# One decode block on one core: wq issued behind ACT's table load, and wider row spacing of two weights in DRAM

## The chip, the core and the metric

The kernel runs on one core of a Trainium2 chip. The metric is the device time of one execution in microseconds (us). All inputs lie in DRAM in layouts that the kernel's own preparation chooses; that preparation is not timed.

## What is computed

One token for each of four sequences passes through a block: a modulated layer norm, attention over the last 2,048 positions of a cache, a gated residual, a second modulated norm, and a gated feed-forward layer. The reference, cut to what matters:

```python
W = 2048                                     # from Sk = 8192
mod = silu(c) @ w_mod                        # (4, 6*512): sa, ca, ga, sb, cb, gb
h = layernorm(x) * (1 + ca) + sa
q = (h @ wq)                                 # 32 heads of 128
p = softmax(q @ k_cache[..., -W:, :].T * 128**-0.5)   # 8 groups of 4 heads share k and v
x = x + ga * ((p @ v_cache[..., -W:, :]) @ wo)
h = layernorm(x) * (1 + cb) + sb
x = x + gb * ((silu(h @ w1) * (h @ w3)) @ w2)
```

Everything is float32. The inputs are some 101 MB, nearly all of it weights and cache that are used once.

## The kernel before

All large inputs are loaded into one SBUF tensor, `ring`, of three slots (`slots`, lines 162 and 163) of 64 KiB per partition. What is loaded, in the order of the program:

- slot 0: `w_mod_a` (line 186), the columns of `w_mod` that the first norm needs, with x and c beside them: 128 rows of 4,128 floats, 16,512 bytes. Issued by SP, the first instruction of its queue.
- slot 1: `wq` (line 188): 128 rows of 16,144 floats, 64,576 bytes. Issued by ACT, the first instruction of its queue and its only transfer. The 240 columns of each row that do not fit beside `GUESTS` are loaded as eight small transfers, the `guests` (lines 202 to 204, 3 rows of 5,760 bytes each), into the tile `p_sb` by SP.
- slot 2: the keys and values of group 0, `kv_in[0]` (line 205), 128 rows of 65,536 bytes, by SP.
- then the other groups (`kv[1]` line 296, `kv[2]` line 329, the rest behind each `group(g)`), each into the slot that the work before has read, and at the end `wo` and the rest of `w_mod`, the last group, `w1`, `w3` and `w2`.

The helper `load` (line 174) issues one transfer per tensor; the source it is given decides the row spacing in DRAM. `Program` (line 44) records every operation with the tiles it touches; `emit` (line 79) derives the waits from these. The engines run their own operations in the order of the text. All operations of the kernel have line 59 in the profile, since `Program` issues them; they are told apart by tiles.

ACT's next instruction after the issue of wq is line 189, `preload_act_table_set`, which loads the table for Exp and Ln. Its first use is the Exp on c (line 240, tile `e`), which needs `w_mod_a`. From `w_mod_a` on, the norm, the modulation (`mod_columns`, `modulate`) and a transpose give `hT`; then the q projection (line 306 on, tiles `s_ps<-ring,hT`) needs `wq`, and `group(0)` (line 350) needs q and `kv_in[0]`.

`_layout` (line 493) lays the inputs out in DRAM. Rows of `w_mod_a` and `wq` stand there one directly behind the other, 16,512 and 64,576 bytes apart.

Of the kernel before, what the change touches and what calls it, by code (L numbers as in the profile page):

```python
# [9 lines left out]
P = 128  # L10
# [6 lines left out]
GUESTS = 240  # L17
# [130 lines left out]
def block_kernel(nc, w_mod_a, wq, guests, kv_in, wo_mod, last_k_wo, last_v, wo, w1, w3, w2, out):  # L148
# [7 lines left out]
    def sb(name, *shape):  # L156
        return nc.alloc_sbuf_tensor(name, (P, *shape), F32).ap()
# [5 lines left out]
    slots = [ring[:, n * 2 * HALF : (n + 1) * 2 * HALF] for n in range(3)]  # L163
# [10 lines left out]
    def load(dst, src, cuts=(0, 1), queue="sync"):  # L174
        step = src.shape[1] // cuts[-1]
        for lo, hi in zip(cuts[:-1], cuts[1:]):
            do(queue, "dma_start", dst[:, lo * step : hi * step], src[:, lo * step : hi * step])
        return dst[:, : src.shape[1]]
# [4 lines left out]

    first = load(slots[0], w_mod_a)
    wma, xt_sb, ct_sb = first[:, :4096], first[:, 4096:4112], first[:, 4112:]
    wq_t = load(slots[1], wq, queue="scalar")
    do("scalar", "preload_act_table_set", "natural_log_exp_and_others")
    kv = [None] * G  # L190


# [52 lines left out]
    xc, sq, h = (sb(n, P) for n in ("xc", "sq", "h"))  # L245
    ss, ln, r0, ve, a, r = (sb(n, 1) for n in ("ss", "ln", "r0", "ve", "a", "r"))
# [246 lines left out]
def _layout(i):  # L493
    import numpy as np

    def a(t):
        return np.ascontiguousarray(t)

    k = i["A_k_cache"][:, :, SK - W :, :].reshape(B, G, NT, 512, DH)
    v = i["A_v_cache"][:, :, SK - W :, :].reshape(B, G, NT, NC, P, DH)  # L500
    wm = i["w_mod"].reshape(4, P, 6, 4, P)
    xc = np.concatenate([i[n].reshape(B, 4, P).transpose(2, 1, 0).reshape(P, 16) for n in ("A_x", "c")], 1)
    w2 = i["B_w2"].reshape(14, P, D)
    wq = a(i["A_wq"].reshape(4, P, G, 512).transpose(1, 2, 0, 3)).reshape(P, 16384)
    guests = np.zeros((2, 12, 6, GUESTS), np.float32)
    for n, (at, lo, hi) in enumerate(GUEST_AT):
        for m in range(2):
            guests[m, lo:hi, n] = wq[at + 32 * m + lo : at + 32 * m + hi, 16384 - GUESTS :]
    wo = a(i["A_wo"].reshape(2, 4, R, P, D).transpose(0, 3, 1, 2, 4)).reshape(2, P, 8192)
    kv = np.concatenate([k.transpose(1, 4, 2, 0, 3).reshape(G, P, 8192), v.transpose(1, 4, 2, 0, 3, 5).reshape(G, P, 8192)], 2)  # L510
    return {
        "w_mod_a": np.concatenate([a(wm[:, :, :2].transpose(1, 0, 3, 2, 4)).reshape(P, 4096), xc], 1),
        "wq": a(wq[:, : 16384 - GUESTS]),
        "guests": guests.reshape(24, 6 * GUESTS),
        "kv_in": kv[: G - 1],
        "wo_mod": np.concatenate([wo[0], a(wm[:, :, 2:].transpose(1, 0, 3, 2, 4)).reshape(P, 8192)], 1),
        "last_k_wo": np.concatenate([kv[G - 1, :, :8192], wo[1, :, :4096]], 1),
        "last_v": a(kv[G - 1, :, 8192:]),
        "wo": a(wo[1, :, 4096:]),
        "w1": a(i["B_w1"].reshape(4, P, FF).transpose(1, 0, 2)).reshape(P, 4 * FF),  # L520
        "w3": a(i["B_w3"].reshape(4, P, FF).transpose(1, 0, 2)).reshape(P, 4 * FF),
        "w2": a(np.stack([w2[4 * j + c] for c, j in CHUNKS], 1)).reshape(P, NF * D),
    }
# [15 lines left out]
```

## Time and profile before

| | |
|---|---|
| time, median of 3 runs (lowest to highest) | 242.15 us (242.04 to 242.48) |
| span of the profiled execution | 240.8 us (1.35 us below the median of the runs) |
| TensorE busy | 148.7 us (62%) |
| VectorE, ACT busy | 56.3 us (23%), 24.1 us (10%) |
| bytes moved, mean rate over the span | 101.39 MB, 421 GB/s |

The span runs from the first to the last instruction in the profile; for the profiled execution itself the profile gives no other time, so the difference to the median of the runs is what lies around the span. PE is TensorE, DVE is VectorE, POOL is GpSimd, SP is the engine that issues most transfers; ACTq and SPq are the queues of ACT and SP, where transfers are issued. DMA share is the mean busy share of the core's 16 DMA engines. Busy shares are averages over stages with different limits, so the stages are read one by one below.

### The profile page before, as it was taken

The page shows a single profiled execution, that of the slowest core. Times are in us where ns is not written, and L with a number is a line of the kernel's source. Part 1 is how long each engine was busy: PE and PEld are TensorE (multiplying, and loading weights), DVE is VectorE, ACT ScalarE, POOL GpSimd, SP SyncE. Part 2 cuts the span into 40 slices and gives each one's busy share as a digit, 9 for nine tenths or more (in the row PEclk, how much of TensorE's full clock was granted, in tenths as well). Part 3 has the DMA queues.
Part 4 walks back from the last instruction along what each step waited for, and adds up shares of the span by engine and source line. Part 5 has one row for each costly group of instructions (what it writes and reads, how often), then busy time and mean ns, then how long its engine had stood idle before and what let it go on. Part 6 is the DMA issues. An engine that isn't in the chain of part 4 may idle for free.

```text
span 240.8 us, 2502 instructions
## 1 busy us (share of the span) xinstructions
PE 148.7 (62%) x1113; PEld 54.2 (22%) x1113; DVE 56.3 (23%) x141; ACT 24.1 (10%) x36; POOL 4.5 (2%) x12
## 2 busy tenths in 40 slices
PE   0000169982984962944867576667399719965876
PEld 0000133322322212201312222221042202422333
DVE  5000231034152024123132133130313104113210
ACT  2000000003003003001100300300200001320100
POOL 7000000000000000000000000000000000000000
PEclk9999997997696798879797799795759968995899
DMA  8999999999999999999999999999999999999994
GB/s 305 434 444 455 424 425 446 416 446 414 457 395 468 403 459 414 449 425 446 425 446 427 435 435 435 435 427 446 425 446 425 411 419 430 386 444 443 401 413 162
DMA packets 2937, 101.39 MB, mean 421 GB/s; under 512 B 472, under 2 KB 472, under 8 KB 880
## 3 DMA queue, kind: packets, MB, share of 16 engines
q1 hardware_dynamic: 2784, 92.99, 89.8%
q10 hardware_dynamic: 144, 8.27, 8.0%
q8 instruction: 8, 0.13, 0.2%
q14 instruction: 1, 0.01, 0.0%
HBM read 101.22 MB, written 0.03 MB: 420 GB/s over the span
## 4 chain that ended last, share of the span: by engine, by line
DMA 60%; PE 31%; DVE 5%; ACT 3%; issue 1%; ACTq 0%
DMA ring<-kv_in 33%; DMA ring<-w 16%; PE s_ps L59 14%; DMA ring<-w_mod_a 11%; PE bank L59 9%; PE o_ps L59 6%; DVE nm L59 3%; ACT p_sb L59 3%; PE a_ps L59 1%; DVE mod_a L59 0%; ACT work L59 0%; DVE p_sb L59 0%; DVE e L59 0%; DVE h L59 0%; DVE sq L59 0%
## 5 line engine op out<-in xcount | busy, mean ns | idle before, releaser
L59 PE MATMUL s_ps<-ring,qT 128*32 128x512 f32 x256 | 36.5, 722 | 20.3 <-DMA ring<-kv_in 13.3
L59 PE MATMUL bank<-ident,p_sb 128*128 128x128 f32 (+1 forms) x136 | 27.7, 353 | 30.8 <-ACT p_sb L59 30.7
L59 PE MATMUL o_ps<-ring,pT 128*16 128x512 f32 x256 | 38.4, 707 | 0.1
L59 PEld LDWEIGHTS bank<-ident,p_sb 128*128 128x128 f32 (+1 forms) x136 | 19.8, 178 | 52.5 <-ACT p_sb L59 31.7
L59 ACT ACTIVATE p_sb<-s_ps,nm 128x2048 f32<-128x2048 f32 (+1 forms) x11 | 16.5, 1501 | 139.7 <-DVE oT L59 104.1
L59 DVE TENSOR_REDUCE nm<-s_ps 128x1 f32<-128x2048 f32 x7 | 16.0, 2292 | 32.5 <-PE s_ps L59 32.5
L59 DVE COPY pT<-bank 128x64 f32<-128x64 f32 x32 | 7.2, 225 | 57.0 <-PE bank L59 57.0
L59 PEld LDWEIGHTS s_ps<-ring,qT 128*32 128x32 f32 x256 | 8.7, 129 | 46.9 <-issue 20.1
L59 PE MATMUL bank<-ident,xs 128*128 128x128 f32 x1 | 0.5, 476 | 27.8 <-POOL xs L59 27.8
L59 PE MATMUL s_ps<-ring,h2T 128*32 128x512 f32 (+1 forms) x64 | 9.0, 657 | 2.3 <-DMA ring<-w 2.3
L59 PE MATMUL s_ps<-ring,hT 128*32 128x512 f32 (+1 forms) x64 | 9.4, 705 | 0.0
L59 PEld LDWEIGHTS o_ps<-ring,pT 128*16 128x16 f32 x256 | 5.4, 99 | 11.9 <-issue 9.0
L59 DVE SCALAR_TENSOR_TENSOR o_own<-o_ps,rl,own 128x512 f32<-128x512 f32 x7 | 5.3, 751 | 11.1 <-PE o_ps L59 11.1
L59 PE MATMUL a_ps<-ring,oT 128*4 128x512 f32 x64 | 7.4, 592 | 0.0
L59 DVE TENSOR_REDUCE o_sum<-o_own 128x128 f32<-128x512 f32 x7 | 7.2, 1034 | 0.2
L59 PE MATMUL bank<-ring,sc 128*32 128x256 f32 (+1 forms) x64 | 6.9, 587 | 0.0
L59 PEld LDWEIGHTS bank<-ident,xs 128*128 128x128 f32 x1 | 0.2, 183 | 27.8 <-POOL xs L59 27.8
L59 DVE TENSOR_SCALAR e<-e 128x16 f32<-128x16 f32 x1 | 0.2, 175 | 23.3 <-ACT e L59 23.3
L59 DVE COPY qT<-bank 128x64 f32<-128x64 f32 x8 | 2.2, 280 | 12.4 <-PE bank L59 12.0
L59 DVE TENSOR_REDUCE mx<-s_ps 128x1 f32<-128x512 f32 x4 | 2.8, 692 | 9.0 <-PE s_ps L59 9.0
L59 PEld LDWEIGHTS s_ps<-ring,h2T 128*32 128x32 f32 x64 | 2.6, 130 | 7.3 <-issue 4.4
L59 PE MATMUL s_ps<-ring,hidT 128*32 128x64 f32 (+1 forms) x112 | 3.6, 274 | 0.3 <-DVE hidT L59 0.3
(97 smaller groups left out, 63.7 us busy)
## 6 DMA issues: line engine op xcount, KB each, us to landing
ring<-wq ACTq DMA_DIRECT2D x1, 8072.0 KB, 26.9
ring<-w SPq DMA_DIRECT2D x2, 3584.0 KB, 37.9
ring<-last_k_wo SPq DMA_DIRECT2D x1, 6144.0 KB, 30.1
ring<-last_v SPq DMA_DIRECT2D x1, 4096.0 KB, 39.5
ring<-w_mod_a SPq DMA_DIRECT2D x1, 2064.0 KB, 26.7
ring<-wo SPq DMA_DIRECT2D x1, 2048.0 KB, 41.8
ring<-w SPq DMA_DIRECT2D x1, 2048.0 KB, 43.1
ring<-w SPq DMA_DIRECT2D x1, 768.0 KB, 44.5
```

Of the source, the lines that this page charges most:

```text
L59: op = Op(engine, lambda: getattr(getattr(self.nc, engine), method)(*args, **kw), [])
```

## The change

Three things. On ACT the issue of `wq` moves from ahead of the table load to behind it. In DRAM the rows of `w_mod_a` are filled up with zeros to 5,120 floats, so that they begin 20,480 bytes apart, and those of `wq` to 17,408 floats, 69,632 bytes apart. The loads take the same 4,128 and 16,144 floats of each row as before, so the same bytes move into the same places.

```diff
-    first = load(slots[0], w_mod_a)
+    first = load(slots[0], w_mod_a[:, :4128])
     wma, xt_sb, ct_sb = first[:, :4096], first[:, 4096:4112], first[:, 4112:]
-    wq_t = load(slots[1], wq, queue="scalar")
     do("scalar", "preload_act_table_set", "natural_log_exp_and_others")
+    wq_t = load(slots[1], wq[:, : 16384 - GUESTS], queue="scalar")
...
+    def spaced(t, row):
+        return np.concatenate([t, np.zeros((P, row - t.shape[1]), np.float32)], 1)
...
-        "w_mod_a": np.concatenate([a(wm[:, :, :2].transpose(1, 0, 3, 2, 4)).reshape(P, 4096), xc], 1),
-        "wq": a(wq[:, : 16384 - GUESTS]),
+        "w_mod_a": spaced(np.concatenate([a(wm[:, :, :2].transpose(1, 0, 3, 2, 4)).reshape(P, 4096), xc], 1), 5120),
+        "wq": spaced(wq[:, : 16384 - GUESTS], 17408),
```

ACT's instructions at the start of the program, with + and - where the change differs from before (`e` is the Exp on c, `ring` the loaded inputs, `ln` the first norm):

```order
@@ -1,4 +1,4 @@
+L59 ACT_TABLE_LOAD
 L59 DMA ring<-wq 128x16144
-L59 ACT_TABLE_LOAD
 L59 ACTIVATE e<-ring 128x16
 L59 ACTIVATE ln<-bank,eps_t 128x1
```

The two first rows have changed places, and nothing else on ACT has moved.

SP's instructions at the start of the program, in the changed kernel:

```order
L59 DMA ring<-w_mod_a 128x4128
L59 DMA p_sb<-guests 3x1440 x8
L59 DMA ring<-kv_in 128x16384 x7
L59 DMA ring<-wo_mod 128x16384
```

They stand as they did before; so do those of TensorE, VectorE and GpSimd.

## Rows read from the trace of the kernel before

**Rows 1.** Page, chain that ended last: start us, us, what; first its shares.
```profile
DMA 60%; PE 31%; DVE 5%; ACT 3%; issue 1%; ACTq 0%
...
0.73 26.68 DMA ring<-w_mod_a
...
67.41 38.51 DMA ring<-kv_in
...
123.18 40.79 DMA ring<-kv_in
...
190.94 38.54 DMA ring<-w
```

**Rows 2.** Windows, two stretches of keys and values (first line: the columns).
```profile
core 0: us, PE busy (x) PEld busy (x) DVE busy (x) ACT busy (x) POOL busy (x), PEclk, DMA share, GB/s
47.25:66.60 19.35, 14.10 (x91) 5.49 (x92) 5.50 (x14) 2.65 (x3) 0.00 (x0) 0.82 1.00 434
...
144.00:163.35 19.35, 11.66 (x82) 4.23 (x82) 5.84 (x10) 2.06 (x2) 0.00 (x0) 0.91 1.00 431
```

**Rows 3.** Timeline of SP's issues to 70 us: start us, us, engine, line, operation.
```profile
8.95 40.08 SPq L59 DMA_DIRECT2D ring<-kv_in  x3
...
34.19 0.33 SPq L59 DMA_DIRECT2D ring<-kv_in  x1
...
48.70 0.33 SPq L59 DMA_DIRECT2D ring<-kv_in  x1
...
67.41 0.33 SPq L59 DMA_DIRECT2D ring<-kv_in  x1
```

**Rows 4.** Windows, the long middle and the last microseconds.
```profile
28.00:229.50 201.50, 139.81 (x945) 49.76 (x944) 51.26 (x118) 21.39 (x32) 0.00 (x0) 0.84 1.00 431
...
236.00:236.50 0.50, 0.50 (x8) 0.12 (x4) 0.00 (x0) 0.00 (x0) 0.00 (x0) 1.00 0.82 328
...
237.00:237.50 0.50, 0.47 (x35) 0.30 (x25) 0.00 (x0) 0.44 (x1) 0.00 (x0) 1.00 0.68 262
237.50:238.00 0.50, 0.50 (x36) 0.50 (x40) 0.00 (x0) 0.00 (x0) 0.00 (x0) 1.00 0.08 29
```

**Rows 5.** Windows, the start: first packets, then one turn of both queues per window.
```profile
1.50:2.50 1.00, 0.00 (x0) 0.00 (x0) 0.96 (x6) 0.93 (x1) 1.00 (x1) 1.00 1.05 264
2.50:3.50 1.00, 0.00 (x0) 0.00 (x0) 1.00 (x9) 0.00 (x0) 1.00 (x3) 1.00 2.64 1033
3.50:5.25 1.75, 0.00 (x0) 0.00 (x0) 0.88 (x4) 0.00 (x0) 1.52 (x3) 1.00 0.00 0
5.25:8.25 3.00, 0.00 (x0) 0.00 (x0) 0.00 (x0) 0.00 (x0) 0.00 (x0) 1.00 1.00 432
...
23.25:26.25 3.00, 0.00 (x0) 0.00 (x0) 0.00 (x0) 0.00 (x0) 0.00 (x0) 1.00 1.00 432
```

**Rows 6.** DMA issues: operation, KB each, median us from issue to landing.
```profile
ring<-wq ACTq DMA_DIRECT2D x1, 8072.0 KB, 26.9
...
ring<-w_mod_a SPq DMA_DIRECT2D x1, 2064.0 KB, 26.7
...
p_sb<-guests SPq DMA_DIRECT2D x8, 16.9 KB
```

**Rows 7.** Timeline of ACT to 30 us; in brackets idle time before, and its releaser.
```profile
0.73 0.39 ACTq L59 DMA_DIRECT2D ring<-wq  x1
1.15 1.28 ACT L59 ACT_TABLE_LOAD   x1 [1.15 <-PEq L532]
27.43 0.21 ACT L59 ACTIVATE e<-ring 128x16 f32<-128x16 f32 x1 [25.00 <-DMA ring<-w_mod_a]
```

**Rows 8.** Chain that ended last, 27 to 54 us: start of q projection and of scores.
```profile
27.43 0.22 ACT e L59
...
36.85 11.81 PE s_ps L59 x76
...
50.60 3.65 PE s_ps L59 x32
```

## The prediction

> **What bounds the kernel now.** I read the chain that ended last first. On the page it is DMA for 60% and TensorE for 31% of the span, and its long pieces are waits for a transfer: 26.68 us for w_mod_a, 38.51 and 40.79 us for two groups of keys and values, 38.54 us for w3 [rows 1]. Such a wait is longer than a transfer. One group is 128 rows of 65,536 bytes, 8.39 MB; the stretches of 19.35 us each move 434 and 431 GB/s with a DMA share of 1.00 [rows 2], so one group needs 8.39 MB / 434 GB/s = 19.3 us, and a wait of 38.5 us is a transfer standing behind another one. That says: the queue is never empty, and TensorE's pieces in the chain lie beside transfers that run anyway.
>
> The issues of SP show how deep the queue is [rows 3]. Its transfers run in order and one at a time from w_mod_a on. The group issued at 67.41 us lands at 67.41 + 38.51 = 105.92 us [rows 1]; counting back by 19.35 us per group, the earlier ones end at 86.6, 67.2 and 47.9 us. So the issue at 34.19 us had 13.7 us in hand before the queue would have run dry, the one at 48.70 us had 18.5 us, the one at 67.41 us had 19.2 us. From 28 us to 229.50 us the DMA share is 1.00 at 431 GB/s [rows 4], and only in the last 2 us do some engines run out of work [rows 4]. The end is therefore: the time at which the transfers reach full rate, plus their bytes at full rate, plus a short tail (last matmuls, two additions, the store of the result). The change moves no byte into or out of the total, so it can act in two ways only: through the rate, and through the first microseconds.
>
> **The first microseconds** [rows 5]. A row of these windows counts a packet where it starts. The window from 1.50 us holds 264 KB, the first row of w_mod_a (16,512 bytes) on each of 16 engines; the next holds 1,033 KB, the first row of wq (64,576 bytes) on each. Their shares, 1.05 and 2.64 over 1.00 us, are the mean time of one such packet: 1.05 and 2.64 us. After that each 3.00 us hold one row of both per engine (432 GB/s x 3.00 us = 1.30 MB = 16 x 81,088 bytes), split by bytes 0.61 and 2.39 us. The two queues thus take turns, row by row, and both transfers need all 8 turns: w_mod_a and wq land 26.7 and 26.9 us after their issues at 0.73 us [rows 6], although w_mod_a has a quarter of the bytes. The start is dear: 1.05 - 0.61 = 0.44 us and 2.64 - 2.39 = 0.25 us, together 0.69 us on a mean engine.
>
> **The change part by part.**
>
> *The issue behind the table load.* The two instructions of ACT swap places; nothing is added. Now the issue takes 0.39 us from 0.73 us and the table load 1.28 us from 1.15 us [rows 7]. Behind the load the issue begins near 0.73 + 1.28 = 2.0 us. What is queued behind it on ACT is only the Exp for silu(c), which waits for w_mod_a until 27.43 us [rows 7]. So the table load itself costs nothing, and the later wq is covered by w_mod_a: 8 rows of 0.61 us per engine keep all engines busy from about 1.7 to 1.7 + 0.44 + 8 x 0.61 = 7.0 us, and wq's first packets started some 2 us after its issue [rows 5, 7]. Only an issue later than 5 us would leave an engine idle.
>
> In 1.28 us two rows of w_mod_a pass (1.28 / 0.61). It then finishes two turns ahead: 2 x 2.39 = 4.8 us earlier, landing at 27.4 - 4.8 = 22.6 us. wq's last two rows take turns with the first rows of the first group of keys and values, which is issued at 8.95 us [rows 3]: 2 x 2.42 us, landing at 27.6 + 4.8 = 32.4 us. The q projection started at 36.85 us after 9.4 us of work from w_mod_a on [rows 8]; it will start at 22.6 + 9.4 = 32.0 us or at wq's landing, so near 32.5 us instead of 36.85 us. That is worth nothing at the end: the scores of group 0 began at 50.60 us [rows 8] and need a group that lands at 47.9 us in either kernel, and the issues that become earlier had 13.7 to 19.2 us in hand already. What is late next is the transfer, as before.
>
> *The start.* With the rows of w_mod_a alone on the engines, the first of them still meets cold engines (0.44 us), but wq's first packet no longer has to come at once: while it is fetched, the second and third rows of w_mod_a fill the time. Nothing in the trace shows a second queue joining a running one, so I bound it: below, the whole 0.69 us goes; above, nothing goes, or the excess comes twice (+0.69 us), since a cold packet of other spacing is not in the trace either. I take the part that belongs to wq, -0.25 us; it is the nearest row.
>
> *The spacing.* Rows 69,632 and 20,480 bytes apart, of the same length as before. Rows 64,576 and 16,512 bytes apart moved 432 GB/s [rows 5] and rows 65,536 bytes apart 431 to 434 GB/s [rows 2]: three spacings, one rate. I cost it at nothing. The bound: 1% of rate over 10.4 MB is 0.24 us either way.
>
> **Sum.** The profiled execution has a span of 240.8 us, 1.35 us below the median of the runs, 242.15 us, and I add that back. 240.8 - 0.25 + 0 + 0 = 240.55 us of span, 241.9 us of time. A measurement of this kernel tells about 0.2% (0.48 us) from no change, so the forecast is called no change.
>
> **The rivals.**
>
> *The order of arrival stays.* ACT's sequencer may hand the table load to the engine and issue wq at once, near 0.8 us. Then two transfers start together as now, the 0.69 us stay and w_mod_a still lands near 27.4 us: 242.15 us, by the spacing at most 0.24 us to either side. For it: the row of the issue stands under ACT's queue, not under the engine [rows 7]; against it: in this trace nothing on ACT is issued behind work of ACT, so it shows neither. The Trainium skill, "Perfetto Trace Analysis", section "DVE / Act Engine Instruction", says that ACT's sequencer is ready for the next instruction once it has pushed the last into a wait queue; by that rule the wait for the table load would not exist. No run here shows whether a table load keeps to it.
>
> *The start is cured whole.* If the cold packets come from two queues fetching at once, or from where the rows lie, all 0.69 us go, on the engines that finish last too: 242.15 - 0.69 = 241.45 us. For it: both first packets are long, not wq's alone [rows 5]. Against it: the first fetch of an idle engine has to wait for memory whatever stands behind it.
>
> *A start that is worse on the engines that end last.* The eight small transfers of guests hold three rows each [rows 6], 5,760 bytes a row; by rows they reach three engines at most, which carry 8 x 5,760 bytes / (434 / 16 GB/s) = 1.7 us more than the others. The falling share at the end [rows 4] fits: some engines finish 1.5 us early. So the end hangs on a few engines, and what one of them loses at the start is never won back. If the new spacing or the later queue doubles their excess, the time is 242.15 + 0.69 = 242.8 us. It decides from 0.48 us on. For it: 0.69 us is a mean, so some engines must already lose more than others. Against it: wq now joins engines that are at work.
>
> **How the numbers follow.** Forecast 0.38, order stays 0.27, cured whole 0.22, worse 0.13. Faster by over 0.2% (below 241.67 us) comes from the cured start and from the edge of the forecast: 0.22 + 0.06 = 0.28. Slower by over 0.2% comes from the worse start, less its small cases: 0.12. No change: 0.60. The range is 241.3 to 242.6 us: the cured start less 0.15 us of spacing below, above the unchanged order with the spread of the runs (0.33 us over the median) and a little of the third rival.
>
> **What would show it.** Right: ACT's issue near 2.0 us; a w_mod_a that lands 20 to 25 us after its issue instead of 26.7 us, and a wq that lands past 30 us; the first packets of wq at 2.4 us each; the groups of keys and values still at 431 to 434 GB/s and the span 0.2 to 0.3 us shorter. The first rival: ACT's issue near 0.8 us and unchanged landings. The second: first packets of w_mod_a at 0.6 to 0.7 us. The third: longer first packets and later groups by the same amount. I am wrong altogether if a DMA share well under 1.00 shows up between 3 and 229 us, or if the rate of wq's stretch falls below 425 GB/s.

## The result, and the profile after

The changed kernel takes 242.88 us (median of 5 runs, 242.64 to 243.5) against 242.15 us: a ratio of 1.0032, 95% interval 1.0021 to 1.0042. It is slower by 0.73 us, outside the range given. The profiled execution took 242.66 us, with a span of 241.3 us.

First ACT, the timeline of the changed kernel, which answers to [rows 7] (start us, us, engine, line, operation):

```profile
0.73 1.28 ACT L59 ACT_TABLE_LOAD   x1 [0.73 <-PEq L535]
0.76 0.38 ACTq L59 DMA_DIRECT2D ring<-wq  x1
27.68 0.21 ACT L59 ACTIVATE e<-ring 128x16 f32<-128x16 f32 x1 [25.66 <-DMA ring<-w_mod_a]
```

The issue of wq did not wait for the table load. It began 0.03 us after the load did and 1.25 us before the load ended, 0.03 us later than in the kernel before. So the two first transfers still take turns from their first rows on, and land together as before; the DMA issues of the changed kernel, against [rows 6]:

```profile
ring<-wq ACTq DMA_DIRECT2D x1, 8072.0 KB, 27.1
...
ring<-w_mod_a SPq DMA_DIRECT2D x1, 2064.0 KB, 26.9
```

Both are 0.2 us later. The windows of the start, against [rows 5], and of the long middle, against [rows 2, 4]:

```profile
core 0: us, PE busy (x) PEld busy (x) DVE busy (x) ACT busy (x) POOL busy (x), PEclk, DMA share, GB/s
1.50:2.50 1.00, 0.00 (x0) 0.00 (x0) 0.95 (x6) 0.52 (x1) 1.00 (x1) 1.00 0.96 264
2.50:3.50 1.00, 0.00 (x0) 0.00 (x0) 1.00 (x9) 0.00 (x0) 1.00 (x3) 1.00 2.50 969
3.50:5.25 1.75, 0.00 (x0) 0.00 (x0) 0.88 (x4) 0.00 (x0) 1.52 (x3) 1.00 0.09 37
5.25:8.25 3.00, 0.00 (x0) 0.00 (x0) 0.00 (x0) 0.00 (x0) 0.00 (x0) 1.00 1.01 432
...
47.25:66.60 19.35, 13.54 (x90) 5.14 (x88) 5.99 (x15) 2.65 (x3) 0.00 (x0) 0.82 1.00 434
144.00:163.35 19.35, 12.96 (x82) 4.50 (x82) 4.09 (x8) 2.06 (x2) 0.00 (x0) 0.82 1.01 434
...
28.00:229.50 201.50, 137.76 (x945) 48.17 (x945) 50.53 (x117) 21.39 (x32) 0.01 (x1) 0.86 1.00 431
```

The rate is what it was: 432 GB/s in a turn of w_mod_a and wq, 431 to 434 GB/s later. The first packets are no longer on the mean either (0.96 us for w_mod_a's; wq's fall into two windows now, since one of the 16 starts after 3.50 us). Yet some start later. Split at 2.20 us, the first window is, in the changed kernel:

```profile
1.50:2.20 0.70, 0.00 (x0) 0.00 (x0) 0.69 (x4) 0.52 (x1) 0.70 (x1) 1.00 0.77 212
2.20:2.60 0.40, 0.00 (x0) 0.00 (x0) 0.37 (x4) 0.00 (x0) 0.40 (x1) 1.00 1.06 289
```

and in the kernel before:

```profile
1.50:2.20 0.70, 0.00 (x0) 0.00 (x0) 0.69 (x4) 0.70 (x1) 0.70 (x1) 1.00 1.43 354
2.20:2.60 0.40, 0.00 (x0) 0.00 (x0) 0.37 (x4) 0.23 (x1) 0.40 (x1) 1.00 0.11 41
```

354 GB/s over 0.70 us are 248 KB, 15 rows of w_mod_a, and 41 GB/s over 0.40 us are one more. After the change it is 9 rows ahead of 2.20 us, and 7 behind.

Whether that matters is seen in the landings. A transfer reports 16 of them, one per engine, and the last counts. In the order of time, from the trace, for the groups kv_in[1] and kv_in[2] (us):

```
before kv_in[1]  65.36 65.42 65.45 65.51 65.52 65.53 65.59 65.64 65.66 66.02 66.08 66.09 67.16 67.17 67.19 67.21
       kv_in[2]  84.72 84.79 84.86 84.87 84.88 84.94 84.99 85.00 85.37 85.42 85.43 86.29 86.51 86.52 86.54 86.56
after  kv_in[1]  65.40 65.47 65.61 65.65 65.69 65.81 65.82 65.83 65.84 66.07 66.22 66.35 67.09 67.24 67.45 67.47
       kv_in[2]  84.75 84.82 84.97 85.00 85.05 85.16 85.17 85.18 85.19 85.41 85.58 86.44 86.60 86.80 86.83 87.20
```

Each engine needs 19.35 us per group, so each number comes again 19.35 us later, unless something else took its engine. Before, the last engine goes 67.21 to 86.56. After, the last engine of kv_in[1] is 0.26 us later (67.47), and a second thing happens: the engine of 66.35 should land at 85.70 and lands at 87.20. In between, at 68.42 us, it served a fetch of instructions, 16 KB, one of the eight that the page counts in both kernels (`q8 instruction: 8`), and that cost it 1.50 us. The packet records show it on the same engine: its row ends at 68.43 us, the fetch takes 0.98 us, and the row behind it takes 2.89 us instead of 2.42 us. Before, the fetch of this stretch met an engine that stood at 65.4 to 65.7 us; the sum, 86.29 us, lies below the last one. So 0.26 us come from the engines that were last already, 0.37 us (87.20 - 86.83) from one that was late by less and met a fetch. The last piece of w2 lands at 238.78 us instead of 238.14 us, 0.64 us later: nothing in between wins any of it back. The last matmuls start as much later, but take 0.15 us less, so that the span grows by 0.51 us; from the chains that ended last, before and after:

```profile
237.49 1.31 PE s_ps L59 x64
238.15 1.16 PE s_ps L59 x64
```

This is one execution. How the two parts come out in other executions and kernels stands behind the table at the end of the experiments.

### The profile page after: what moved, and what is told of

The parts are those of the page before. It is cut to its first block, busy times and chain, and to the rows that moved or that the text cites. A ratio compares the mean times of both kernels' runs of the same rounds, so it can differ in the third digit from the quotient of the medians.

```text
span 241.3 us, 2502 instructions
## 1 busy us (share of the span) xinstructions
PE 146.3 (61%) x1113; PEld 52.4 (22%) x1113; DVE 56.2 (23%) x141; ACT 24.1 (10%) x36; POOL 4.5 (2%) x12
## 4 chain that ended last, share of the span: by engine, by line
DMA 76%; PE 18%; DVE 3%; ACT 2%; issue 0%; SPq 0%
DMA ring<-kv_in 31%; DMA ring<-wo_mod 17%; DMA ring<-w 16%; DMA ring<-w_mod_a 11%; PE bank L59 6%; PE s_ps L59 6%; PE o_ps L59 4%; ACT p_sb L59 2%; DVE nm L59 2%; PE a_ps L59 1%; DVE p_sb L59 0%; DVE e L59 0%; DVE sq L59 0%; DVE xc L59 0%; DVE tot L59 0%
## 5 line engine op out<-in xcount | busy, mean ns | idle before, releaser
L59 PE MATMUL s_ps<-ring,qT 128*32 128x512 f32 x256 | 37.2, 734 | 22.0 <-DMA ring<-kv_in 15.0
L59 PE MATMUL bank<-ident,p_sb 128*128 128x128 f32 (+1 forms) x136 | 26.3, 338 | 30.8 <-ACT p_sb L59 30.7
L59 PE MATMUL o_ps<-ring,pT 128*16 128x512 f32 x256 | 37.6, 693 | 0.0
L59 PEld LDWEIGHTS bank<-ident,p_sb 128*128 128x128 f32 (+1 forms) x136 | 18.5, 169 | 51.7 <-ACT p_sb L59 31.7
L59 PE MATMUL bank<-ident,xs 128*128 128x128 f32 x1 | 0.5, 476 | 28.1 <-POOL xs L59 28.1
L59 PE MATMUL s_ps<-ring,h2T 128*32 128x512 f32 (+1 forms) x64 | 9.6, 693 | 1.4 <-DMA ring<-w 1.1
L59 PE MATMUL s_ps<-ring,hT 128*32 128x512 f32 (+1 forms) x64 | 7.7, 588 | 0.0
L59 PEld LDWEIGHTS bank<-ident,xs 128*128 128x128 f32 x1 | 0.2, 183 | 28.1 <-POOL xs L59 28.1
## 6 DMA issues: line engine op xcount, KB each, us to landing
ring<-wq ACTq DMA_DIRECT2D x1, 8072.0 KB, 27.1
ring<-w_mod_a SPq DMA_DIRECT2D x1, 2064.0 KB, 26.9
```

Source lines behind the costliest of these rows:

```text
L59: op = Op(engine, lambda: getattr(getattr(self.nc, engine), method)(*args, **kw), [])
```

## Experiments

Each kernel was timed against the kernel before, in five rounds; "span" is the median over its executions, where the kernel before has 240.9 us.

**Which part costs it.** The swap alone (rows packed), the spacing alone (ACT's order as before), and both kernels once more, as they stand.

```diff
-    wq_t = load(slots[1], wq, queue="scalar")
     do("scalar", "preload_act_table_set", "natural_log_exp_and_others")
+    wq_t = load(slots[1], wq, queue="scalar")
```

> The swap on ACT alone, rows packed as before. Theory A (the spacing costs the time): wq is still issued at 0.76 us beside w_mod_a, so 242.15 us, within 0.2 us. Theory B (the swap costs it, by the order in which the two issues reach the DMA engines): 242.7 to 243.0 us, as the whole change. Theory C (the start of each engine is drawn anew in each execution, whatever the kernel): anywhere from 242.0 to 243.5 us, with a spread over its own runs as wide as the changed kernel's 0.9 us.

242.22 us, ratio 1.0001 (0.9992 to 1.0009), span 240.9 us. The swap costs nothing. Its timeline shows the issue beside the table load, with packed rows too:

```profile
0.73 1.28 ACT L59 ACT_TABLE_LOAD   x1 [0.73 <-PEq L532]
0.76 0.38 ACTq L59 DMA_DIRECT2D ring<-wq  x1
27.28 0.22 ACT L59 ACTIVATE e<-ring 128x16 f32<-128x16 f32 x1 [25.26 <-DMA ring<-w_mod_a]
```

```diff
+    wq_t = load(slots[1], wq[:, : 16384 - GUESTS], queue="scalar")
     do("scalar", "preload_act_table_set", "natural_log_exp_and_others")
-    wq_t = load(slots[1], wq[:, : 16384 - GUESTS], queue="scalar")
```

(against the changed kernel)

> The spacing of 69632 and 20480 bytes alone, ACT's order as before. Theory A (spacing): 242.7 to 243.0 us, and kv_in[0]'s last engine lands at 48.1 us or later instead of 47.87 us. Theory B (swap): 242.15 us. Theory C (a draw): spread of 0.9 us over its own runs.

242.78 us, ratio 1.0026 (1.0015 to 1.0037), span 241.3 us, executions from 242.45 to 244.02 us. Theory A stands: the spacing carries the cost, the whole 0.4 us of span that the changed kernel has over the kernel before in its repeated runs. Its four late first rows of w_mod_a are in the window 2.20 to 2.60 us (165 GB/s over 0.40 us = 66 KB):

```profile
1.50:2.20 0.70, 0.00 (x0) 0.00 (x0) 0.69 (x4) 0.70 (x1) 0.70 (x1) 1.00 1.16 283
2.20:2.60 0.40, 0.00 (x0) 0.00 (x0) 0.37 (x4) 0.23 (x1) 0.40 (x1) 1.00 0.54 165
```

> The kernel before, once more, for a second profile of its start. Theories A and B: 242.15 us within 0.15 us, and the landings of each transfer on the 16 engines are as in the first profile (guests' last engine at 28.5 us, kv_in[0]'s at 47.9 us). Theory C: the late engines of the start differ, the last landing of kv_in[0] moves by 0.2 us or more.

242.23 us, span 240.9 us; kv_in[0] lands last at 47.92 us (47.87 us in the first profile). Theory C falls for this kernel.

> The changed kernel once more. Theories A and B: 242.6 to 243.0 us, kv_in[0] landing last at 48.1 us again. Theory C: a time between 242.1 and 243.5 us that need not lie above the kernel before.

243.81 us, ratio 1.0052 (1.0034 to 1.0070), span 241.3 us; kv_in[0] lands last at 48.07 us. The span is that of the first profile of it (241.3 us); the time is higher, above what was expected, since 4 of 6 executions lie at 243.7 to 244.0 us. I come back to these.

**Which tensor, and is it the place in DRAM.** One tensor spaced at a time; and rows packed, but with zeros behind the last row, so that the tensors are as large as the spaced ones.

```diff
-        "wq": a(wq[:, : 16384 - GUESTS]),
+        "wq": spaced(wq[:, : 16384 - GUESTS], 17408),
```

(in part; against the kernel before, with `spaced` and the load's slice as in the change; this is the edit for wq alone, the one for w_mod_a alone is the other line of the change)

> Only w_mod_a's rows 20480 bytes apart; wq packed, ACT's order as before. If the late first packets of the spaced kernels (four engines whose first row of w_mod_a starts after 2.2 us, where the packed kernels have one) come from w_mod_a's spacing, they show here and the span is 241.1 to 241.6 us, the time 242.5 to 242.9 us. If they come from wq's spacing or from the size of the tensors: span 240.8 us and 242.15 us.

242.41 us, ratio 1.0019 (1.0007 to 1.0031), span 241.05 us.

> Only wq's rows 69632 bytes apart. If w_mod_a's spacing is the cause: 242.15 us, one late first packet, span 240.8 us. If wq's is: span 241.1 to 241.6 us, 242.5 us or more.

242.44 us, ratio 1.0013 (1.0005 to 1.0021), span 241.1 us. Neither expectation came: each tensor has a part in it, about 0.15 and 0.2 us of span, together close to the 0.4 us of both.

The number of late first rows does not go with the cost. In the traces, 2 of w_mod_a's 16 first rows start after 2.20 us with w_mod_a spaced, and 1 with wq spaced, as in the kernel before; the next kernel, which costs nothing, has 3. With wq spaced the engines are done with their last rows of wq by 26.99 us (before: 27.05 us), but the three engines of guests begin these at 26.40, 26.55 and 26.65 us instead of 26.33, 26.33 and 26.36 us. What differs there is which engines are late, not how late they are.

```diff
+    def longer(t, rows):
+        return np.concatenate([t, np.zeros((rows - P, t.shape[1]), np.float32)], 0)
...
+        "w_mod_a": longer(np.concatenate([a(wm[:, :, :2].transpose(1, 0, 3, 2, 4)).reshape(P, 4096), xc], 1), 159),
+        "wq": longer(wq[:, : 16384 - GUESTS], 138),
```

(in part; the loads take the first 128 rows)

> Rows packed as before, but zeros behind the last row, so that both tensors take as many bytes of DRAM as the spaced ones and everything behind them is moved as far. If the distance between rows is the cause: 242.15 us. If only where the tensors lie in DRAM is: 242.5 us or more, and some executions with over 1.3 us more than span plus 1.35 us, as two of the spaced kernels had.

242.26 us, ratio 1.0001 (0.9993 to 1.0010), span 240.9 us. It is the distance between rows, not the size of the tensors nor where those behind them lie.

**What about the distance.** Three other pairs of distances, ACT's order as before; against the spacing alone, the two numbers of `spaced` are all that differs:

```diff
-        "w_mod_a": spaced(np.concatenate([a(wm[:, :, :2].transpose(1, 0, 3, 2, 4)).reshape(P, 4096), xc], 1), 5120),
-        "wq": spaced(wq[:, : 16384 - GUESTS], 17408),
+        "w_mod_a": spaced(np.concatenate([a(wm[:, :, :2].transpose(1, 0, 3, 2, 4)).reshape(P, 4096), xc], 1), 5152),
+        "wq": spaced(wq[:, : 16384 - GUESTS], 18192),
```

and 8192 and 32768, and 9216 and 33792 floats.

> Both spaced, but 20608 and 72768 bytes apart: the rows then begin at the same steps within 4096 bytes as the packed rows do (128 and 3136 bytes further with each row), while those of the change all begin at the same place within 4096 bytes. If the late starts come from rows that begin alike: span 240.9 us as before, 242.2 us. If any gap between the rows costs: span 241.2 to 241.4 us, 242.5 to 242.8 us.

242.44 us, ratio 1.0015 (1.0004 to 1.0026), span 241.1 us: between the two expectations. Rows that begin at different places within 4096 bytes, as packed rows do, are not free.

> Both spaced, 32768 and 131072 bytes apart. If rows that begin alike are what makes engines start late, this is worse than the change: guests' last landing after 28.8 us, span 241.4 us or more. If any gap costs the same: span 241.2 to 241.4 us. If the rate itself suffers from such a distance: windows of a turn longer than 3.00 us, some us in all.

242.31 us, ratio 1.0003 (0.9994 to 1.0012), span 241.0 us, and 432 GB/s in a turn. These gaps, wider than those of the change and with all rows beginning alike, cost nothing clear of the noise. So it is neither any gap nor rows that begin alike.

> Both spaced, 36864 and 135168 bytes apart, 4096 bytes more than the powers of two that cost nothing. If distances of an odd number of 4096 bytes are what costs: span 241.2 to 241.4 us. If it is something of the particular distances of the change: 240.9 to 241.0 us.

242.38 us, ratio 1.0010 (1.0001 to 1.0019), span 241.1 us. This lies between the two expectations, and its interval overlaps with that of the powers of two. Which property of a distance decides stays open.

**How a late start reaches the end.** The eight transfers of guests left out, in the kernel before and in the changed one; the last 240 columns of each row of wq then count as zero.

```diff
-    for m in range(2):
-        for c in range(4):
-            do("sync", "dma_start", guest[32 * m + c : 32 * m + 12 : 4], guests[12 * m + c : 12 * m + 12 : 4])
```

> Kernel before without the eight transfers of guests: the last 240 columns of each row of wq count as zero. Prediction's picture (three engines carry 1.7 us more than the others and set the end alone): the span falls by 1 us or more, to 239.9 us or less. Rival (eight other engines lose about as much to the fetches of instructions, so that eleven engines end together): the span falls by 0.3 us at most, 240.6 us or more.

242.07 us, ratio 0.9992 (0.9984 to 1.0001), span 240.7 us: 0.2 us, not 1 us. The three engines with guests do not set the end alone. The end windows of this kernel, against [rows 4], show the share falling further ahead of the end, and the end staying:

```profile
236.00:236.50 0.50, 0.50 (x8) 0.13 (x4) 0.00 (x0) 0.00 (x0) 0.00 (x0) 1.00 0.76 283
...
237.00:237.50 0.50, 0.48 (x36) 0.32 (x24) 0.00 (x0) 0.47 (x1) 0.00 (x0) 1.00 0.40 156
237.50:238.00 0.50, 0.48 (x34) 0.48 (x38) 0.00 (x0) 0.00 (x0) 0.00 (x0) 1.00 0.05 16
```

> The changed kernel without the eight transfers of guests (the last 240 columns of each row of wq count as zero). If the spacing costs time because the three engines that carry guests start later, the cost goes with the guests: span 240.7 us, as the kernel before without guests. If the engines that meet instruction fetches start later as well: 240.9 to 241.1 us. If every engine starts later: 241.1 us, the whole 0.4 us more.

242.50 us, ratio 1.0012 (1.0003 to 1.0021), span 241.2 us, 0.5 us above the kernel before without guests. The cost does not go with the guests; of the three expectations the last, the whole 0.4 us, is nearest. But its reason, that every engine starts later, is not in the profile: kv_in[0] lands at 46.34 us on the mean in both kernels without guests, and its last landing is earlier in the slower one (47.65 us instead of 47.95 us). What the profile has is again an engine that met a fetch: it was at 66.21 us in kv_in[1] and is last in kv_in[2] at 87.08 us, where the engine that had been last, 67.03 us, is due at 86.38 us. One profile can't tell whether the distance or chance brings the fetch to such an engine; how the change costs its 0.5 us here stays open.

**Is the intended order worth anything.** Packed rows, and wq's issue really held, by a small clearing of its place on GpSimd that the issue must wait for.

```diff
-    wq_t = load(slots[1], wq, queue="scalar")
...
     do("gpsimd", "memset", p_all[:44], 0.0)
+    do("gpsimd", "memset", slots[1][:, :16], 0.0)
+    wq_t = load(slots[1], wq, queue="scalar")
```

> Packed rows; wq's issue really is held, by a small clearing of its place on GpSimd, to some 3.3 us. My forecast's term, that wq's first packets no longer cost 0.25 us: w_mod_a lands 15 to 21 us after its issue, wq's first packets take 2.4 us on the mean instead of 2.6, the span falls by 0.2 to 0.3 us, 241.9 us. Rival, that the start is the engines' first fetch and nothing else: w_mod_a lands earlier all the same, but the span stays at 240.8 us. Rival, that guests or keys that meet wq's last rows cost something: slower than 242.3 us.

242.57 us, ratio 1.0018 (1.0010 to 1.0027), span 241.25 us. Issue, landings and first packets, from its timeline, its DMA issues and its windows:

```profile
3.29 0.37 ACTq L59 DMA_DIRECT2D ring<-wq  x1
13.09 0.22 ACT L59 ACTIVATE e<-ring 128x16 f32<-128x16 f32 x1 [11.07 <-DMA ring<-w_mod_a]
```

```profile
ring<-wq ACTq DMA_DIRECT2D x1, 8072.0 KB, 38.6
...
ring<-w_mod_a SPq DMA_DIRECT2D x1, 2064.0 KB, 12.3
```

```profile
1.50:2.50 1.00, 0.00 (x0) 0.00 (x0) 0.95 (x6) 0.52 (x1) 1.00 (x1) 1.00 1.37 264
...
6.80:7.50 0.70, 0.00 (x0) 0.00 (x0) 0.00 (x0) 0.00 (x0) 0.00 (x0) 1.00 3.41 1476
```

w_mod_a lands 14.4 us earlier, earlier than expected, and the Exp starts at 13.09 us, and the end gains nothing by it, as forecast. wq's first packets take 0.70 x 3.41 = 2.39 us: their 0.25 us are gone, as forecast. But now w_mod_a's first packets take 1.37 us instead of 1.05 us: over 0.61 and 2.39 us, the start costs 0.76 us on a mean engine here, and 0.69 us before. The span is longer, not shorter, and the last landing of kv_in[0] is at 48.30 us instead of 47.87 us. That is the mark of the second rival of the expectation, slower than 242.3 us: the rows of guests, in the trace at 26.3 to 28.1 us before, run between rows of wq from 9.8 us on here, and kv_in[0] meets wq's last rows. No run parts these from the start, so what made the held kernel slower stays open.

**The executions near 244 us.**

> The changed kernel a third time. The span is 241.3 us on the median again, and the last landing of kv_in[0] lies at 48.0 to 48.2 us. The executions with more than 1.6 us around the span, 4 of 6 in one run of it and none of 5 in the other: if they belong to the kernel, some are here too; if they belonged to that chip, none.

243.22 us, ratio 1.0045 (1.0023 to 1.0068), span 241.3 us. Of 8 executions 4 are at 243.8 to 244.3 us. Over the three runs of the changed kernel it is 9 of 19 above 243.4 us, with the spacing alone 2 of 11, with w_mod_a spaced, wq spaced, 20608 and 72768 bytes, or wq held one of 12 each, and none of 11 in each of the kernels with the swap alone, the longer tensors, the powers of two, 36864 and 135168 bytes, or without guests, nor in any execution of the kernel before. Three such executions were profiled (changed kernel again, spacing alone, 20608 and 72768 bytes), and all three have a ninth fetch of instructions near the end, at 243.0, 242.6 and 240.7 us, in the first two behind the last instruction of the span; the other profiles have eight. In the third it fell on the store of the result; its page's DMA row and SP's waits:

```profile
q8 instruction: 9, 0.15, 0.2%
```

```profile
SPq L145 <- DMA out<-p_sb: 2.7, 1, 2.7
```

SP waited 2.7 us for the store, where the kernel before waits 1.0 us; 15 engines had landed by 241.01 us and one at 242.65 us. Why there is a ninth fetch in some executions was not tried. These executions raise the medians of two of the three runs of the changed kernel above the first; that all of them have a ninth fetch is not shown, since only three were profiled.

The last landings, one profile per kernel (us; guests, kv_in[0], and the last piece of w2):

```
                        guests  kv_in[0]  w2      span, median
before                   28.48   47.87   238.14   240.9
before again             28.55   47.92   238.25   240.9
swap alone               28.46   47.87   238.12   240.9
longer tensors           28.55   47.91   238.51   240.9
32768 and 131072         28.54   47.90   238.28   241.0
w_mod_a spaced           28.65   48.01   238.46   241.05
wq spaced                28.77   48.13   238.40   241.1
20608 and 72768          28.71   48.07   238.51   241.1
36864 and 135168         28.67   48.18   238.46   241.1
wq held                  28.93   48.30   238.61   241.25
both spaced              28.68   48.04   238.71   241.3
the change               28.76   48.12   238.78   241.6
the change again         28.72   48.07   238.62   241.3
the change, third time   28.73   48.31   238.58   241.3
```

Of these kernels, every one at 240.9 or 241.0 us has its guests in by 28.55 us and kv_in[0] by 47.92 us; every slower one is later in both. (The two kernels without guests, above, do not follow this.) The mean over the 16 engines does not part them: for kv_in[6] it is 163.24 us before, 163.17 us with the swap alone, 163.22 us with both spaced, 163.18 us with w_mod_a spaced; for the change it is 163.27 to 163.40 us.

The two parts behave differently. From the last landing of kv_in[0] to that of w2 it takes 190.25 to 190.28 us before, with the swap alone, with wq spaced, with 36864 and 135168 bytes and in the third run of the change: there a late kv_in[0] is the whole loss (0.44 us in the third run). In the second run of the change 0.20 us come from kv_in[0] and 0.28 us later; with the longer tensors, which are packed, nearly nothing from kv_in[0] (0.04 us) and 0.33 us later. So in these profiles the late kv_in[0] goes with the spacing (and with wq held), while what is added behind it is met in a packed kernel too. That the distance between rows moves lateness onto the engines that end last is the reading that fits; by which step it does so no run shows.

## Why the prediction was wrong

*What bounds the kernel*: right. The queue never ran dry, the rates are 431 to 434 GB/s in both kernels, and moving w_mod_a's landing by 14 us (wq held) gained nothing at the end.

*"Behind the load the issue begins near 0.73 + 1.28 = 2.0 us"*: this step failed first. The issue begins at 0.76 us. The first rival, that the order of arrival stays, had it right with 0.8 us, and the landings of 26.9 and 27.1 us are its landings. The rule of the Trainium skill that stood beside it ("Perfetto Trace Analysis", "DVE / Act Engine Instruction"), that the sequencer is ready for the next instruction once it has pushed the last into the wait queue, agrees with the trace: ACT's sequencer began the issue 0.03 us after the table load had begun. What hung on the 2.0 us, the landing of w_mod_a at 22.6 us and of wq at 32.4 us, did not come. By itself this step would have left the time at 242.15 us, as the swap alone shows (242.22 us).

*"I take the part that belongs to wq, -0.25 us"*: wrong as a price too. With wq held, its part goes and w_mod_a's part grows from 0.44 to 0.76 us; the span rises by 0.35 us. In this kernel the excess of the first packets was not saved by holding one transfer back.

*"Three spacings, one rate. I cost it at nothing"*: this step put the time out of the range. The rate was right, also for the new distances, and the cost was not in the rate. The spacing alone costs 0.4 us of span and 0.6 us of time (242.78 us); with packed rows of as many bytes it is gone (242.26 us). In the profiles with guests it shows as later last landings of guests and kv_in[0]. The bound that I gave, 1% of rate, bounded the wrong thing.

*The third rival*, a start that is worse on the engines that end last, forecast 242.8 us and 0.13 of chance; 242.88 us was measured. Its core holds: the end hangs on the engines that end last, and what they lose early is not won back. But its own sign, longer first packets, did not come (0.96 us instead of 1.05 us on the mean), and two of its parts were off. It named three engines, those with guests; without guests the end moves by 0.2 us only, since the engines that serve instruction fetches (some 1.5 us each) end with them: in the kernel before, eleven of the 16 land the last piece of w2 between 237.81 and 238.14 us. And the later queue, one of its two causes, did not exist; the spacing alone did it. Its 0.69 us were a doubled mean; what was measured in the profiled execution is 0.26 us on the last engines and 0.37 us from an engine that met a fetch, and the executions near 244 us put more on the medians. That 242.8 us came so near to the measured 242.88 us is luck.

The chances were wrong in their order: I read a mean (0.69 us) where the end hangs on the last of 16 engines, and so called the rival that worked with single engines the least likely.

## What to carry to other kernels

Where transfers follow one another without a gap, what one DMA engine loses in the first microseconds is still there at the end: compare the 16 landings of an early transfer, last against last, since the mean rate and the mean start show nothing, and then look for what joins the last engine later on. An issue that stands behind a table load of the same engine in the program need not wait for it; if it is to wait, give it something to wait for. And a layout in DRAM is to be timed by itself, each tensor alone, even where its rows move at full rate.

## What was not expected of the hardware

- A fetch of 16 KB of instructions cost the engine that served it 1.50 us (66.35 to 87.20 us less 19.35 us), and 1.64 us in the store of the result; at the rate of one engine, 434 / 16 GB/s, 16 KB would be 0.6 us, by estimate.
- Rows 20480 and 69632 bytes apart cost 0.4 us of span, rows 32768 and 131072 bytes apart 0.1 us, which is not clear of the noise, although all four move 432 GB/s once they move.
- With the second transfer held back, the first packets of the first one were slower, 1.37 us instead of 1.05 us, in the one profile of it.
